# Long convolution with a dense layer: product on VectorE, shared buffers in both stages of the convolution, wider weight split

## The chip, the core and the metric

The kernel runs on one core of a Trainium2 chip. Five engines work side by side, each through its own list of instructions in order: TensorE (PE, matrix products, with the loading of weights shown apart as PEld), VectorE (DVE), ScalarE (ACT), GpSimd (POOL) and SyncE (SP), which here only starts transfers (DMA). An instruction waits until what it needs is there, and everything behind it on its engine waits with it. The metric is the device time of one execution in microseconds, less is better.

## The reference

Two steps, with a batch of 4, a sequence S of 12480 and a width D of 128. The convolution runs along the sequence with a filter that a small network makes from position embeddings; the dense layers (called MoE in the names) follow on each of the 49920 tokens, with 2048 inner columns.

```python
h_filt = (np.maximum(pos_emb @ w1, 0.0) @ w2) * np.exp(-0.01 * pos)[:, None]
u = x * v
Uf = np.fft.rfft(u, n=2 * S, axis=1)
Hf = np.fft.rfft(h_filt, n=2 * S, axis=0)
y = np.fft.irfft(Uf * Hf[None], n=2 * S, axis=1)[:, :S, :]
a = (x * y).reshape(B * S, D)
g = np.maximum(a @ w_in, 0.0) ** 2
return g @ w_out
```

Inputs and result are float32; the weights of the dense layers arrive as 64-bit floats, whose bits the kernel splits on the chip into a high and a low part that TensorE can multiply.

## The kernel before

The transform over 90 x 128 points is done as matrix products, in four quarters q of 32 channels each. A quarter has two stages.

**Stage one** has 20 chunks c. The first 16 hold signal: the tiles x and v (98 x 1024, 392 KB each) are loaded by SP (`load_c`, L161, with x in 4 and v in 3 buffers), POOL multiplies them (`prep`, L176), DVE makes the sums and differences u (L179), PE multiplies u by the transform matrix (`s1_quad`, pss, L196, 32 rows of the profile a chunk), and ACT copies the result to P (L199, two a chunk). The last 4 chunks hold the filter, loaded as four tiles f from the DRAM tensor fd (L166), whose parts DVE and ACT copy to u (L185). `load_c` runs three chunks ahead, `prep` two chunks, across the border of a quarter too.

In quarter 0 the filter itself is made beside chunks 0 to 7: four groups a chunk, each with the product psm1 (L125) on 64 partitions, a relu on ACT (L127), the product psm2 (L134), the window on DVE (ft, L136) and sums and differences on DVE and POOL (feo, L145), which `store_f` stores to fd.

Beside stage one the 64-bit weights are split (`weights`): a part of CW = 256 columns (tile raw, L228) is loaded by SP, DVE takes it apart in 14 operations on tiles cv (L233 to L250), and wst goes to the DRAM tensor wd (L252). Sixteen parts make four a quarter. The generator runs in pieces, one in each of several chunks.

**Stage two** has 30 steps z a quarter. PE multiplies P by wt (psx, L270; wt loaded by SP, L258), ACT copies a part (hs, L274), DVE multiplies (two tiles t, L278), POOL makes the two halves of y (L286, L287), PE multiplies again (psc, L295), ACT copies (ci, L297), DVE makes cs (L299, L300), and SP stores it to the DRAM tensor cd (L301). The second half of a step (`i2`, from psc on) runs two steps late, through the list todo; the last two of a quarter run after the next quarter's stage one.

**Stage three** goes back through the transform (psy, pst) and through the dense layers (psh, L467, and pso, L493). It takes the time from about 842 us on. What it needs first (the inverse transform's iwt, x3, the weights wi and wo from wd) is loaded during the last second stage.

The order on each engine is written by hand (a manual schedule): instructions stand there as the Python code emits them. Tiles come from pools; a tile that takes a used buffer waits for the last user of that buffer.

Of the kernel before, what the change touches and what calls it, by code (L numbers as in the profile page):

```python
# [66 lines left out]
CW = 256  # L67
# [12 lines left out]
def conv_moe(ctx, tc, xc, vc, xg, pos, win, w1, w2, ew, fw, ident_d, sw, iw, iw0, w_in, w_out, out):  # L80
# [23 lines left out]
    with ExitStack() as c1:  # L104
        big = c1.enter_context(tc.tile_pool(name="big", bufs=1, side="right"))
        low = ExitStack()
        s1 = low.enter_context(tc.tile_pool(name="s1", bufs=3))
# [7 lines left out]
        def load_f(i):  # L115
            if i < NG // FG:
                pt = wf.tile([FO, FG, G2 * RF], F32, tag="pos", name="pt")
                sp.dma_start(pt, pos[i])
                sf["pos", i] = pt

        def filt(g):
            if g >= NG:
                return
            ps = psM.tile([FO, G2 * RF], F32, tag="m1", name="psm1")
            pe.matmul(ps, lhsT=w1_sb, rhs=sf["pos", g // FG][:, g % FG], start=True, stop=True)  # L125
            h1 = wf.tile([FO, G2, RF], F32, tag="h1", name="h1")
            act.activation(h1.rearrange("p a b -> p (a b)"), ps, AF.Relu)  # L127
            sf["h", g] = h1

        def filt2(g):  # L130
            h1 = sf.pop(("h", g))
            ps = psM.tile([RF, G2, D], F32, tag="m2", name="psm2")
            for j in range(G2):
                pe.matmul(ps[:, j], lhsT=h1[:, j], rhs=w2_sb, start=True, stop=True)  # L134
            ft = wf.tile([RF, G2, D], F32, tag="ft", name="ft")
            dve.tensor_tensor(  # L136
                ft, ps, win_sb[:, G2 * g : G2 * g + G2].unsqueeze(2).broadcast_to([RF, G2, D]), op=ALU.mult
            )
            i, j = g // FG, 2 * (g % FG)
            if j == 0:  # L140
                sf["eo", i] = wf.tile([RF, 2, Q, 2 * FG, QC], F32, tag="feo", name="feo")
            ft = ft.rearrange("p j (q d) -> p j q d", q=Q)
            for e, op in enumerate((ALU.add, ALU.subtract)):
                fe = sf["eo", i][:, e, :, j : j + 2].rearrange("p q j d -> p j q d")
                (dve, pool)[e].tensor_tensor(fe, ft[:, :2], ft[:, 2:], op=op)  # L145

        def store_f(i):
            fe = sf.pop(("eo", i))
            for e in range(2):
                sp.dma_start(fd[:, :, e, 2 * FG * i : 2 * FG * (i + 1)].rearrange("n q j d -> n q (j d)"),  # L150
                             fe[:, e].rearrange("n q j d -> n q (j d)"))


        def load_c(g):
            q, c = divmod(g, NC)
            if q >= Q or c > NU:
                return
            if c < NU:
                for n, src in enumerate((xc, vc)):
                    ch[g, n] = s1.tile([R1, 8 * N2], F32, tag="xv"[n], name="xv"[n], bufs=4 - n)  # L160
                    sp.dma_start(ch[g, n], src[q, c])  # L161
                return
            for e in range(2):
                for h in range(2):
                    t = s1.tile([R1, 8 * N2], F32, tag="xv"[e], name=f"f{e}", bufs=4 - e)
                    sp.dma_start(t[:RF], fd[:, q, e, 32 * h : 32 * (h + 1)].rearrange("n j d -> n (j d)"))  # L166
                    ch["f", e, h] = t[:RF].rearrange("n (j d) -> n d j", d=QC)

        def prep(g):
            q, c = divmod(g, NC)  # L170
            if q >= Q:
                return
            u = s1.tile([R1, 8, N2], F32, tag="u", name="u")
            if c < NU:
                x, v = (ch.pop((g, n)) for n in range(2))
                pool.tensor_tensor(x, x, v, op=ALU.mult)  # L176
# [3 lines left out]
            else:  # L180
                d = 8 * (c - NU)
                for e, copy in enumerate((dve.tensor_copy, act.copy)):
                    for h in range(2):
                        j = e * H2 + 32 * h
                        copy(u[:RF, :, j : j + 32], ch["f", e, h][:, d : d + 8])  # L185
# [22 lines left out]
        nums = const.tile([128, 16], U32, tag="num", name="nums")  # L208
# [4 lines left out]
        def weights(i):  # L213
# [12 lines left out]
            else:  # L226
# [4 lines left out]
                t, sg, m, rest = (s1.tile([128, CW], U32, tag=f"cv{n}", name=f"cv{n}", bufs=1) for n in range(4))  # L231
                shl, shr = ALU.logical_shift_left, ALU.logical_shift_right
                dve.scalar_tensor_tensor(t, wh, 1, num(21), op0=shl, op1=shr)  # L233
# [3 lines left out]
                dve.scalar_tensor_tensor(sg, wh, 31, num(31), op0=shr, op1=shl)  # L237
                dve.scalar_tensor_tensor(sg, t, 23, sg, op0=shl, op1=ALU.bitwise_or)
# [4 lines left out]
                dve.scalar_tensor_tensor(rest, wl, 3, num(9), op0=shl, op1=shr)  # L243
                dve.tensor_tensor(rest, rest, sg, op=ALU.bitwise_or)
                fr, fm = rest.bitcast(F32), m.bitcast(F32)
# [15 lines left out]
        def s2(z):  # L261
# [14 lines left out]
            for c in range(2):  # L276
                t = s2p.tile([N2, 6, B, QC], F32, tag=f"t{c}", name=f"t{c}", bufs=2)
# [373 lines left out]
```

## Time and profile before

| | us |
|---|---|
| median of 3 runs | 3168.01 (3164.02 to 3176.44) |
| the profiled execution | 3183.8 |
| its span in the profile | 3181.9 |
| quarter 0: stage one, stage two | 0 to 181.8, to 270.3 |
| quarter 1 | to 357.2, to 448.1 |
| quarter 2 | to 532.3, to 623.2 |
| quarter 3 | to 706.5, to 812.8 |
| first products of stage three | about 842 |

The borders are read from the timeline of PE, where pss gives way to psx and psc, and back. Busy shares over the whole span: PE 96%, DVE 76%, ACT 66%, POOL 27%. These are averages over stages with different limits, so the stages are looked at one by one. In the rows of the profile each group has its line, engine, operation, the tile written and the tiles read, the shape, the count, the busy time and mean duration, and the idle time of the engine just ahead of it with what ended it. In a table of stretches each engine has its busy time and, in brackets, its number of instructions; PEclk is the clock that TensorE was granted, as a share of the full one.

### The profile page before, as it was taken

How to read it: one execution, taken by the hardware profiler on the slowest of the kernel's cores; microseconds unless marked ns; L12 is line 12 of the kernel's file. 1: busy time of each engine (PE TensorE's matmuls, PEld its weight loads, DVE VectorE, ACT ScalarE, POOL GpSimd, SP SyncE). 2: the span in 40 equal slices, each digit the busy share in tenths (PEclk: the TensorE clock that was granted, in tenths of full speed). 3: DMA queues.
4: the chain of work that ended last, by engine and by line, in shares of the span. 5: the costliest groups of instructions: out<-in, count | busy, mean ns of one | idle time of the engine just before them, and what ended most of it. 6: DMA issues, size and time to landing. Idle time of an engine off the chain costs nothing.

```text
span 3181.9 us, 42191 instructions
## 1 busy us (share of the span) xinstructions
PE 3058.0 (96%) x15370; PEld 2472.3 (78%) x15370; DVE 2433.7 (76%) x2853; ACT 2097.4 (66%) x2634; POOL 852.2 (27%) x662
## 2 busy tenths in 40 slices
PE   8997988978799999999999999999999999999999
PEld 5676767767688888888888888888888888888887
DVE  3688888888677777777777777777777777777776
ACT  2243434343477777777777787777777777777776
POOL 3456464646221111121121121111211121111210
PEclk7798999989899999999999999999999999999999
DMA  5567676757421112221121221221221222211110
GB/s 149 160 183 204 182 205 188 208 167 243 118 73 58 51 58 63 66 61 58 51 63 58 67 59 51 58 63 56 70 58 52 58 63 64 62 58 52 58 36 14
DMA packets 205807, 291.75 MB, mean 92 GB/s; under 512 B 13470, under 2 KB 131616, under 8 KB 205088
## 3 DMA queue, kind: packets, MB, share of 16 engines
q1 hardware_dynamic: 196240, 262.96, 28.5%
q0 software_dynamic: 9360, 26.10, 3.0%
q8 instruction: 122, 2.00, 0.3%
q14 instruction: 85, 0.70, 0.1%
HBM read 205.77 MB, written 83.23 MB: 91 GB/s over the span
## 4 chain that ended last, share of the span: by engine, by line
PE 88%; DVE 6%; DMA 3%; issue 1%; ACT 1%; POOL 1%; SPq 0%; DVEq 0%; POOLq 0%; ACTq 0%
PE psh L467 34%; PE pso L493 33%; PE psx L270 6%; PE psy L436 5%; PE psc L295 5%; PE pss L196 3%; DVE u L179 2%; PE pst L453 1%; PE psm L134 1%; PE psm L125 1%; DMA f<-fd 1%; DMA wt<-in_sw_dram 1%; DMA raw<-in_w_out_dram 1%; DVE cv L237 0%; ACT P L199 0%
## 5 line engine op out<-in xcount | busy, mean ns | idle before, releaser
L88 DVE TENSOR_TENSOR glo<-gt,ghi 128x1024 fp32r<-128x1024 f32 (+1 forms) x784 | 1090.5, 1391 | 60.6 <-DVE ghi L479 1.4
L470 ACT ACTIVATE rt<-psh 128x1024 f32<-128x1024 f32 (+1 forms) x784 | 800.8, 1021 | 401.1 <-PE psh L467 386.4
L479 DVE CAST ghi<-gt 128x1024 fp32r<-128x1024 f32 (+1 forms) x784 | 540.9, 690 | 470.6 <-ACT gt L477 469.6
L493 PE MATMUL pso<-ghi,wo 128*128 128x512 f32 (+1 forms) x3136 | 858.0, 390 | 0.0
L467 PE MATMUL psh<-xhi,wi 128*128 128x512 f32 (+1 forms) x3136 | 856.8, 395 | 0.6 <-ACT xhi L85 0.4
L477 ACT ACTIVATE gt<-rt 128x1024 f32<-128x1024 f32 (+1 forms) x784 | 829.3, 1058 | 23.8 <-DVE glo L88 0.4
L88 POOL TENSOR_TENSOR clo<-ca,chi 128x512 fp32r<-128x512 f32 x126 | 225.3, 1788 | 1746.7 <-ACT chi L85 1184.8
L493 PEld LDWEIGHTS pso<-ghi,wo 128*128 128x128 f32 x3136 | 588.4, 188 | 124.8
L467 PEld LDWEIGHTS psh<-xhi,wi 128*128 128x128 f32 x3136 | 580.2, 188 | 120.8 <-ACT xhi L85 0.6
L493 PE MATMUL pso<-glo,wo 128*128 128x512 f32 (+1 forms) x1568 | 500.7, 390 | 0.0
L467 PE MATMUL psh<-xlo,wi 128*128 128x512 f32 (+1 forms) x1568 | 484.4, 390 | 0.0
L467 PEld LDWEIGHTS psh<-xlo,wi 128*128 128x128 f32 x1568 | 294.7, 188 | 65.4
L493 PEld LDWEIGHTS pso<-glo,wo 128*128 128x128 f32 x1568 | 294.2, 188 | 64.8
L196 PE MATMUL pss<-e_sb,u 98*64 98x180 f32 (+1 forms) x2560 | 262.2, 361 | 72.1 <-DVE u L179 66.4
L196 PEld LDWEIGHTS pss<-e_sb,u 98*64 98x64 f32 (+1 forms) x2560 | 215.7, 157 | 117.8 <-issue 52.5
L199 ACT COPY P<-pss 128x720 f32<-128x720 f32 x160 | 126.6, 796 | 205.3 <-PE pss L196 205.3
L278 DVE TENSOR_TENSOR t<-psx,hs 128x768 f32<-128x768 f32 x240 | 218.3, 953 | 46.7 <-PE psc L295 33.8
L270 PEld LDWEIGHTS psx<-P,wt 128*128 128x128 f32 x1440 | 212.7, 188 | 45.6 <-issue 12.5
L270 PE MATMUL psx<-P,wt 128*128 128x160 f32 x1440 | 221.8, 302 | 13.4 <-DMA wt<-in_sw_dram 8.0
L274 ACT COPY hs<-psx 128x192 f32<-128x192 f32 x240 | 65.2, 323 | 236.2 <-PE psx L270 234.4
L176 POOL TENSOR_TENSOR x<-x,v 98x1024 f32<-98x1024 f32 x64 | 160.6, 2511 | 143.7 <-DMA v<-in_vc_dram 103.1
L88 POOL TENSOR_TENSOR clo<-cb,chi 104x512 fp32r<-104x512 f32 x126 | 166.4, 1321 | 111.4 <-ACT chi L85 95.0
(54 smaller groups left out, 2180.5 us busy)
## 6 DMA issues: line engine op xcount, KB each, us to landing
cd<-cs SPq DMA_DIRECT2D x120, 384.0 KB
cb<-cd SPq DMA_DIRECT2D x128, 208.0 KB
iwt<-in_iw_dram POOLq DMA_DIRECT2D x65, 392.0 KB, 3.4
x<-in_xc_dram SPq DMA_DIRECT2D x64, 392.0 KB
v<-in_vc_dram SPq DMA_DIRECT2D x64, 392.0 KB
x<-in_x_dram SPq DMA_DIRECT2D x128, 196.0 KB
out_dram<-os SPq DMA_DIRECT2D x48, 512.0 KB
wt<-in_sw_dram SPq DMA_DIRECT2D x120, 192.0 KB
```

The lines of the kernel that those rows point to most:

```text
L88: eng.tensor_tensor(dst, src, hi.bitcast(F32), op=ALU.subtract)
L176: pool.tensor_tensor(x, x, v, op=ALU.mult)
L196: pe.matmul(pv[p, a], lhsT=u[:rows, 4 * h + a, p], rhs=e_sb[:rows, e : e + 2].rearrange("n c k -> n (c k)"), start=True, stop=True)
L270: pe.matmul(xp[:, 3 * c + i, :SIG], lhsT=wt[:, i], rhs=sl["P"][:, c * (N1 // 2) + kp, :, t], start=True, stop=True)
L278: dve.tensor_tensor(t, xp[:, :, : B * QC].rearrange("p m (b d) -> p m b d", b=B), hs[:, c].rearrange("p r k d -> p (r k) d").unsqueeze(2). ...
L295: pe.matmul(cp[c], lhsT=f_sb[:, c], rhs=y[:, c], start=True, stop=True)
L436: pe.matmul(yp, lhsT=lhs, rhs=rhs, start=n == 0, stop=n == len(ops) - 1)
L467: pe.matmul(ps[:, j, :n], lhsT=wi[wp][:, f * 128 : (f + 1) * 128], rhs=bl[b][dp][:, j * n : (j + 1) * n], start=(wp, dp) == TERMS[0], stop ...
L470: act.activation(rt, ps[:, :, :n], AF.Relu)
L477: act.activation(gt, rt, AF.Square)
L479: dve.tensor_copy(hi, gt)
L493: pe.matmul(un["o"][j], lhsT=wo[tm[0]][:, f], rhs=g[tm[1]][:, j], start=f == 0 and tm == TERMS[0], stop=f == NF - 1 and tm == TERMS[-1])
```

## The change

Six edits, all ahead of stage three:

1. The product x * v goes from POOL to DVE.
2. The tiles x, f0, t0 and t1 share five buffers (tag "x"), and v, f1, y and cs share five others (tag "v"), from a pool that lives through both stages. u has 4 buffers where it had 3.
3. `load_c` runs up to five chunks ahead within a quarter. The next quarter's chunks 0 to 2 are loaded in steps 24, 26 and 28 of stage two, and its first two preparations stand in steps 26 and 28. Before, they stood in the last chunks of stage one.
4. The filter takes two groups at a time on 128 partitions: w1 stands twice on the diagonal of a 128 x 128 matrix, and psm2 reads the upper and the lower half of h1 in turn. feo has one buffer for each of sum and difference.
5. CW = 512: eight parts, two a quarter, 13 operations on DVE and the high part's copy on ACT, in pieces of one or two operations over eight chunks.
6. All four u copies of a filter chunk are ACT's. The transfers for stage three are placed anew: ident, wi and the first iwt at the start of the last second stage, wo between the first two loads of stage three; iwt has 2 buffers where it had 3.

```diff
-CW = 256
+CW = 512
...
-        s1 = low.enter_context(tc.tile_pool(name="s1", bufs=3))
+        s1 = low.enter_context(tc.tile_pool(name="s1", bufs=4))
+        mix = c1.enter_context(tc.tile_pool(name="mix", bufs=5, side="right"))
+        def buf(tag, name):
+            return mix.tile([128, 8 * N2], F32, tag=tag, name=name)
...
-            ps = psM.tile([RF, G2, D], F32, tag="m2", name="psm2")
+            ps = [psM.tile([RF, G2, D], F32, tag="m2", name="psm2") for _ in range(2)]
             for j in range(G2):
-                pe.matmul(ps[:, j], lhsT=h1[:, j], rhs=w2_sb, start=True, stop=True)
+                for h in range(2):
+                    r = slice(h * FO, (h + 1) * FO)
+                    pe.matmul(ps[h][:, j], lhsT=h1[r, j], rhs=w2_sb[r], start=True, stop=True)
...
-                    ch[g, n] = s1.tile([R1, 8 * N2], F32, tag="xv"[n], name="xv"[n], bufs=4 - n)
+                    ch[c, n] = buf("xv"[n], "xv"[n])[:R1]
...
-                pool.tensor_tensor(x, x, v, op=ALU.mult)
+                dve.tensor_tensor(x, x, v, op=ALU.mult)
...
-                for e, copy in enumerate((dve.tensor_copy, act.copy)):
+                for e in range(2):
                     for h in range(2):
                         j = e * H2 + 32 * h
-                        copy(u[:RF, :, j : j + 32], ch["f", e, h][:, d : d + 8])
+                        act.copy(u[:RF, :, j : j + 32], ch["f", e, h][:, d : d + 8])
...
                 dve.tensor_tensor(m, m, sg, op=ALU.bitwise_or)
-                dve.scalar_tensor_tensor(rest, wl, 3, num(9), op0=shl, op1=shr)
-                dve.tensor_tensor(rest, rest, sg, op=ALU.bitwise_or)
+                yield
+                act.copy(hi, fm)
+                dve.scalar_tensor_tensor(t, wl, 3, num(9), op0=shl, op1=shr)
+                dve.tensor_tensor(t, t, sg, op=ALU.bitwise_or)
+                yield
...
-                dve.tensor_tensor(hi, fm, fm, op=ALU.max)
...
-                t = s2p.tile([N2, 6, B, QC], F32, tag=f"t{c}", name=f"t{c}", bufs=2)
+                t = buf("x", f"t{c}")[:, : 6 * B * QC].rearrange("p (m b d) -> p m b d", m=6, b=B)
...
-            y = s2p.tile([N2, 2, 3 * B * QC], F32, tag="y", name="y")
+            y = buf("v", "y")[:, : 6 * B * QC].rearrange("p (c w) -> p c w", c=2)
...
-            cs = s2p.tile([N2, 2, 3 * B * QC], F32, tag="cs", name="cs")
+            cs = buf("v", "cs")[:, : 6 * B * QC].rearrange("p (c w) -> p c w", c=2)
...
+                for c in (3, 4):
+                    load_c(q, c)
                 for c in range(NC):
-                    g = q * NC + c
-                    load_c(g + 3)
-                    if c % 5 == 0:
-                        last, part, wpart = part, weights(wpart), wpart + 1
-                    if c % 5 == 1:
-                        next(last, 0)
-                    if c % 5 < 4:
-                        next(part, 0)
+                    if c + 5 <= NU:
+                        load_c(q, c + 5)
+                    if c % 10 == 0:
+                        part, wpart = weights(wpart), wpart + 1
+                    next(part, 0)
...
-                    prep(g + 2)
-                    s1_quad(g, 0)
-                    s1_quad(g, 1)
+                    if c + 2 < NC:
+                        prep(c + 2)
+                    s1_quad(c, 0)
+                    s1_quad(c, 1)
...
+                    if q < Q - 1 and s in (26, 28):
+                        prep(s // 2 - 13)
+                    if q < Q - 1 and s in (24, 26, 28):
+                        load_c(q + 1, s // 2 - 12)
...
             load3(0)
+            for i in range(2):
+                sp.dma_start(wo[i].rearrange("p c d -> p (c d)").bitcast(F32), wd[1, i])
             load3(1)
```

How this moves instructions is seen on three engines at the border from quarter 0's second stage to quarter 1's first stage, and in that stage's last chunks. The first is DVE at the border, before: t and cs belong to the last steps of stage two, u is chunk 2, cv the first weight part.

```order
255 L278 TENSOR_TENSOR t_2066<-psx,hs 128x768
256 L278 TENSOR_TENSOR t_2068<-psx,hs 128x768
257 L299 TENSOR_TENSOR cs<-psc_2073,ci 128x384
258 L300 TENSOR_TENSOR cs<-psc_2073,ci 128x384
259 L179 TENSOR_TENSOR u<-x 98x8x64 x2
260 L233 SCALAR_TENSOR_TENSOR cv_2119<-raw,nums 128x256
261 L235 SCALAR_TENSOR_TENSOR cv_2119<-cv_2119,nums 128x256
```

The same border on DVE after the change; the first two rows are the preparation of chunk 1, the rows ahead of cv that of chunk 2.

```order
237 L180 TENSOR_TENSOR x<-x,v 98x1024
238 L183 TENSOR_TENSOR u<-x 98x8x64 x2
239 L284 TENSOR_TENSOR t_1981<-psx,hs 128x768
240 L284 TENSOR_TENSOR t_1983<-psx,hs 128x768
241 L305 TENSOR_TENSOR cs<-psc_1988,ci 128x384
242 L306 TENSOR_TENSOR cs<-psc_1988,ci 128x384
243 L180 TENSOR_TENSOR x<-x,v 98x1024
244 L183 TENSOR_TENSOR u<-x 98x8x64 x2
245 L237 SCALAR_TENSOR_TENSOR cv_2042<-raw,nums 128x512
246 L238 SCALAR_TENSOR_TENSOR cv_2042<-cv_2042,nums 128x512
```

A preparation now stands between the last steps of stage two, and the first use of raw stands on DVE ahead of every preparation from chunk 3 on.

The second place is SP at the same border, before: the store of step 27, then chunk loads with raw among them. The waits name the counters of engines and of DMA queues that the transfer waits for.

```order
141 L301 DMA cd<-cs 256x3x128 [waits DMAHW4_49,DVE_49]
142 L161 DMA x<-in_xc_dram 98x1024 [waits DMAHW5_49]
143 L161 DMA v<-in_vc_dram 98x1024 [waits DMAHW6_49,Activation_49]
144 L228 DMA raw<-in_w_in_dram 128x512 [waits DMAHW7_49]
145 L161 DMA x<-in_xc_dram 98x1024 [waits DMAHW0_49]
146 L161 DMA v<-in_vc_dram 98x1024 [waits DMAHW1_49,Pool_49]
```

And SP there after the change.

```order
144 L307 DMA cd<-cs 256x3x128 [waits DMAHW7_49,DVE_49]
145 L168 DMA x<-in_xc_dram 98x1024 [waits DMAHW0_49,Pool_49]
146 L168 DMA v<-in_vc_dram 98x1024 [waits DMAHW3_49,DMAHW1_49,Activation_49]
147 L168 DMA x<-in_xc_dram 98x1024 [waits DMAHW2_49]
148 L168 DMA v<-in_vc_dram 98x1024 [waits DMAHW5_49,DVE_49]
149 L168 DMA x<-in_xc_dram 98x1024 [waits DMAHW4_49,Pool_49]
150 L168 DMA v<-in_vc_dram 98x1024 [waits DMAHW7_49]
151 L231 DMA raw<-in_w_in_dram 128x1024 [waits DMAHW6_49]
```

Raw, twice as long, has moved from behind one pair of chunk loads to behind three; the wait of row 148 on DVE is for the product of chunk 2.

The third place is ACT in the last chunks of that first stage, before: u copies of the filter and P copies.

```order
110 L199 COPY P<-pss 128x4x90x2 x28
111 L185 COPY u<-f_2514 96x8x32
112 L185 COPY u<-f_2516 96x8x32
113 L199 COPY P<-pss 128x4x90x2 x2
114 L185 COPY u<-f_2514 96x8x32
115 L185 COPY u<-f_2516 96x8x32
```

And after the change, where wst is the high part of the weight split.

```order
106 L202 COPY P<-pss 128x4x90x2 x18
107 L189 COPY u<-f_2339 96x8x32
108 L189 COPY u<-f_2341 96x8x32
109 L189 COPY u<-f_2343 96x8x32
110 L189 COPY u<-f_2345 96x8x32
111 L202 COPY P<-pss 128x4x90x2 x2
112 L249 CAST wst<-cv_2349 128x512
113 L189 COPY u<-f_2339 96x8x32
```

Four u copies stand ahead of each pair of P copies, where two stood.

More of the change, by code (lines that the diff above doesn't have):

```diff
@@ L147, in store_f @@
         def store_f(i):
-            fe = sf.pop(("eo", i))
-            for e in range(2):
+            for e, fe in enumerate(sf.pop("eo")):
                 sp.dma_start(fd[:, :, e, 2 * FG * i : 2 * FG * (i + 1)].rearrange("n q j d -> n q (j d)"),
[L151 to L157, printed above, removed]
+                             fe.rearrange("n q j d -> n q (j d)"))
@@ L207, in conv_moe @@
         NUM = (0, 9, 21, 31, 254)
-        nums = const.tile([128, 16], U32, tag="num", name="nums")
+        nums = const.tile([128, 24], U32, tag="num", name="nums")
         def num(v):
@@ L322, in conv_moe @@
                 pool.memset(nums[:, i : i + 1], v)
-            w1_sb = load("w1", [FO, FO], w1)
+            w1_sb = load("w1", [2 * FO, 2 * FO], w1)
             load_f(0)
-            w2_sb = load("w2", [FO, D], w2)
+            w2_sb = load("w2", [2 * FO, D], w2)
+            load_f(1)
             win_sb = load("win", [RF, N2], win)
-            load_c(0)
-            load_f(1)
+            load_c(0, 0)
             e_sb = load("e", [R1, 3, N1], ew)
-            load_c(1)
-            load_c(2)
+            load_f(2)
+            load_c(0, 1)
+            load_c(0, 2)
             f_sb = load("f", [N2, 2, N2], fw)
-            ident = load("id", [R1, R1], ident_d)
             filt(0)
-            for g in range(2):
-                prep(g)
+            for c in range(2):
+                prep(c)
             part, wpart = iter(()), 0
@@ L380, in conv_moe @@
                     todo.append(z)
-                    if q == Q - 1 and 4 <= s < 8:
-                        h, i = divmod(s - 4, 2)
-                        sp.dma_start((wi[i], wo[i].rearrange("p c d -> p (c d)"))[h].bitcast(F32), wd[h, i])
-                    if q == Q - 1 and s in (8, 9):
-                        load3_w(s - 8)
+                    if q < Q - 1 and s in (26, 28):
+                        prep(s // 2 - 13)
+                    if q < Q - 1 and s in (24, 26, 28):
+                        load_c(q + 1, s // 2 - 12)
             while todo:
                 i2(todo.pop(0))
+    w4 = ctx.enter_context(tc.tile_pool(name="p3w4", bufs=2))
+    wo = [w4.tile([128, NF, D], F32R, tag=f"wo{i}", name=f"wo{i}", bufs=1) for i in range(2)]
     io3 = ctx.enter_context(tc.tile_pool(name="p3io", bufs=2, side="right"))
+    st3 = {}
     def load3(p):
-        if p not in st3:
-            load3_w(p)
         ca = io3.tile([128, 2, W], F32, tag="ca", name="ca")
@@ L402, in load3 @@
             sp.dma_start(cb[q * CB : (q + 1) * CB], im[M:])
-        st3[p].update(ca=ca, cb=cb)
+        wt = w0
+        if p:
+            wt = [w4.tile([128, 2, 4, R1], F32R, tag="w", name="iwt")]
+            pool.dma_start(wt[0], iw[p])
+        xt = w4.tile([R1, 2, W], F32, tag="x", name="x3")
+        for j, n2 in enumerate(_pair(p)):
+            sp.dma_start(xt[:, j], xg[n2])
+        st3[p] = dict(ca=ca, cb=cb, w=wt, x=xt)
     with ExitStack() as c3:
@@ L503, in conv_moe @@
             load3(0)
+            for i in range(2):
+                sp.dma_start(wo[i].rearrange("p c d -> p (c d)").bitcast(F32), wd[1, i])
             load3(1)
@@ L623 @@
     moe = [a.view(np.int64) if a.dtype == np.float64 else a for a in moe]
+    w1b = np.zeros((2 * FO, 2 * FO), np.float32)
+    w1b[:FO, :FO] = w1b[FO:, FO:] = w1
     ins = dict(
```

112 lines of the change are left out of this document (52 added, 60 removed).

## The prediction

> **What bounds the kernel now.** I read the page first, then the table of stretches cut at the borders of the stages, then groups and timeline of the stretches that the change touches.
>
> ```profile
> span 3181.9 us, 42191 instructions
> PE 88%; DVE 6%; DMA 3%; issue 1%; ACT 1%; POOL 1%; SPq 0%; DVEq 0%; POOLq 0%; ACTq 0%
> core 0: us, PE busy (x) PEld busy (x) DVE busy (x) ACT busy (x) POOL busy (x), PEclk, DMA share, GB/s
> 48.00:92.00 44.00, 44.00 (x182) 27.64 (x182) 14.52 (x27) 8.26 (x14) 16.40 (x14) 0.50 0.46 131
> 92.00:137.00 45.00, 43.42 (x240) 28.93 (x238) 23.55 (x42) 10.86 (x18) 20.99 (x18) 0.70 0.51 147
> 137.00:181.80 44.80, 34.84 (x370) 28.50 (x367) 39.06 (x57) 23.17 (x32) 16.82 (x7) 0.92 0.67 200
> 270.30:357.20 86.90, 64.22 (x642) 53.88 (x641) 75.80 (x99) 34.97 (x47) 43.65 (x19) 0.80 0.68 202
> 357.20:448.10 90.90, 89.89 (x484) 73.17 (x482) 81.52 (x119) 31.58 (x91) 56.56 (x58) 1.00 0.67 183
> 448.10:532.30 84.20, 63.96 (x642) 53.68 (x641) 72.66 (x98) 35.04 (x47) 42.65 (x19) 0.84 0.71 208
> 623.20:706.50 83.30, 62.80 (x641) 52.30 (x641) 70.16 (x96) 35.26 (x47) 38.06 (x17) 0.86 0.63 183
> 706.50:812.80 106.30, 94.26 (x490) 74.10 (x488) 84.63 (x124) 32.39 (x93) 60.73 (x63) 1.00 0.75 224
> ```
>
> PE ends the chain, but from 842 us on nothing is changed. What can move is the first 842 us: four first stages (0 to 181.8 with the filter, then the rows of 86.9, 84.2 and 83.3 us) and four second stages. The second stages are PE's (89.89 busy of 90.9). The first stages are not: PE works 64.22 of 86.9 us, DVE 75.80.
>
> **Product on VectorE.** Part of DVE's 75.80 us is a wait that counts as work:
>
> ```profile
> 283.57 0.42 DVE L237 SCALAR_TENSOR_TENSOR cv<-raw,nums 128x256 uint32<-128x256 uint32 x1
> 284.36 2.56 DVE L239 SCALAR_TENSOR_TENSOR cv<-raw,nums 128x256 uint32<-128x256 uint32 x1
> 284.07 2.57 POOL L176 TENSOR_TENSOR x<-x,v 98x1024 f32<-98x1024 f32 x1 [1.62 <-DMA v<-in_vc_dram]
> L176 POOL TENSOR_TENSOR x<-x,v 98x1024 f32<-98x1024 f32 x16 | 41.3, 2583 | 41.0 <-DMA v<-in_vc_dram 36.7 <-DVE cv L249 3.4 <-DVE cv L244 0.8
> 276.07 1.29 DVE L179 TENSOR_TENSOR u<-x 98x512 f32<-98x512 f32 x2 [3.55 <-POOL x L176]
> 1505.61 1.23 DVE L88 TENSOR_TENSOR glo<-gt,ghi 128x1024 fp32r<-128x1024 f32 x1
> 1506.78 0.69 DVE L498 COPY os<-pso 128x512 f32<-128x512 f32 x1
> ```
>
> The same kind of cv operation takes 0.42 us alone and 2.56 beside POOL's product. A DVE operation on two 1024-wide inputs took 1.23 us with POOL idle, so a preparation (product and both u) costs DVE 1.23 + 1.29 = 2.52 us, with no POOL left in stage one. A weight operation on 512 columns lies between 0.42 (256 wide) and 1.23 (1024); I take 0.69, the row of width 512. Two parts of 13 come to 18 us a quarter, against four parts of 14 before at 0.42, 23.5 us without waits. DVE's work for a first stage is then 14 preparations, 35.3 us, and 18: 53 us. By that alone stage one would lose some 25 us. The queue order takes it back.
>
> **Stage one of quarters 1 to 3**, from its old start (t = 0):
>
> ```profile
> 266.80 1.82 DVE L278 TENSOR_TENSOR t<-psx,hs 128x768 f32<-128x768 f32 x2 [0.22 <-PE psc L295]
> ...
> 269.77 1.82 DVE L278 TENSOR_TENSOR t<-psx,hs 128x768 f32<-128x768 f32 x2 [0.22 <-PE psc L295]
> 271.97 0.55 DVE L300 TENSOR_TENSOR cs<-psc,ci 128x384 f32<-128x384 f32 x1
> L286 POOL TENSOR_TENSOR y<-t,t 128x384 f32<-128x384 f32 x29 | 29.0, 1002 | 35.6 <-DVE t L278 34.2 <-PE psx L270 1.4
> 274.70 0.38 SPq L228 DMA_DIRECT2D raw<-in_w_in_dram  x1
> 280.99 1.75 DVE L233 SCALAR_TENSOR_TENSOR cv<-raw,nums 128x256 uint32<-128x256 uint32 x1 [3.62 <-DMA raw<-in_w_in_dram]
> GB/s 180 201 234 279 268 272 270 279 74 43 321 6 268 223 223 298 307 264 173 204 145 4 0 190 252 293 319 309 172 4 40 288 248 350 255 166 0 185 239 247
> ```
>
> 1. DVE ended stage two at 272.5, t = 2.2. Preparations 0 and 1 now stand in stage two, where DVE waits only 0.22 us in a step, and beside POOL's y (1.00 us each); I charge one y each: 2 x 3.5 = 7.0. DVE ends at 9.2 and preparation 2 at 11.7. Without meeting a y it is 2 us less, with two y each 2 us more. The buffers that y, cs and v now share make the y of the last steps wait for a cd store issued one or two steps (2.97 us, start to start of the t rows) before; I cost that at nothing, and 3 us a stage if the store is late.
> 2. The first raw part is twice as large and stands on SP behind the cd store of step 27, six chunk loads, and v waits for product 2. Store and loads (0.38 + 6 x 0.40 MB) and raw (0.52 MB) are 3.3 MB; at the 270 GB/s of the slices that is 12.2 us from about t = 5, and some 3.5 us for issues and waits: 21. Before, it landed 6.3 us after issue (274.70 to 280.99). Bounds: no stall, or 12 us. I take 9.3, since SP is in order. Behind it on DVE stands every later preparation; PE has two chunks in hand.
> 3. Chunks 1 to 7: 13 x 0.69 and 7 x 2.52 = 26.6, to 47.6. Three without weights: 55.2.
> 4. The second raw part stands behind the v that waits for product 12 (t = 53.9): issue 54.3, landing 60.6 by the same 6.3 us, 5.4 lost. Bounds 0 and 9.
> 5. Product 14, for which the last f load waits: 60.6 + 4 x 0.69 + 2.52 + 1.23 = 67.1. Half the f loads are then already in; the last takes about 3.7 (between 1.5 us of its own 0.38 MB at 270 GB/s and the 5.9 below): 70.8.
> 6. The tail behind the last f:
>
> ```profile
> 336.07 1.25 SPq L166 DMA_DIRECT2D f<-fd  x3
> 342.93 0.63 ACT L185 COPY u<-f 96x256 f32<-96x256 f32 x1 [0.46 <-DMA f<-fd]
> 357.14 1.24 PE L295 MATMUL psc<-y,f_sb 128*128 128x384 f32 x3
> L185 ACT COPY u<-f 96x256 f32<-96x256 f32 x8 | 4.9, 651 | 0.5 <-DMA f<-fd 0.5
> L199 ACT COPY P<-pss 128x720 f32<-128x720 f32 x39 | 31.0, 799 | 51.2 <-PE pss L196 51.2
> ```
>
> It took 14.3 us (342.93 to 357.2), ACT nearly without a break: four times two u copies of 0.65 and some twelve P copies of 0.80 are 14.8. Now ACT makes all four u copies of a chunk: 8 x 0.65 = 5.2 more, 19.5. The stage ends at 90.3, against 86.9, 84.2 and 83.3: +3.4, +6.1, +7.0, **+16.5** together. Deeper loads don't enter: y(28) and y(29) hold two of the five v slots until stage two goes on, so the v of a chunk still waits for the product three chunks earlier.
>
> **Quarter 0.**
>
> ```profile
> 92.45 0.86 PE L125 MATMUL psm<-pt,w_sb 64*64 64x384 f32 x2
> 93.24 1.11 PE L134 MATMUL psm<-w_sb,h 64*96 64x128 f32 x8
> 118.46 1.54 PE L125 MATMUL psm<-pt,w_sb 64*64 64x384 f32 x2
> 119.93 2.02 PE L134 MATMUL psm<-w_sb,h 64*96 64x128 f32 x8
> ```
>
> PE is full from 48 to 137 us (44.00 and 43.42 busy), DVE is not: here only PE's work counts. A psm1 of a group takes 0.79 us at full clock (start to start) and 1.47 at the granted half. Two of four a chunk go: 1.6 or 2.9 us, at the mix of these rows (granted 0.50, then 0.70) about 2.4; seven such chunks **-17**. With the clock at full throughout, these would fall by 36 in all; if the pairs of psm2 wait for ft, since one pair takes both buffers, by 5. Behind them DVE (39.06 of 44.8) sets the pace: by steps 3 to 6, six preparations, a raw stall and the longer tail take about 40: **-5** (0 to -9).
>
> The single feo buffer makes the first feo of a chunk wait for the fd store of the chunk before; a chunk's pss, 2.67 to 4.3 us (rows under B), lies between, so 0.
>
> **The rest.**
>
> ```profile
> L270 PE MATMUL psx<-P,wt 128*128 128x160 f32 x1440 | 221.8, 302 | 13.4 <-DMA wt<-in_sw_dram 8.0
> ```
>
> The last second stage takes 106.3 us against 90.9: psx waits for wt loads, 8.0 of it in this group, that stand behind the bulk loads for stage three. w_out now goes elsewhere, so half of the 8.0 goes: -4. The transition pays for it: w_out (2.1 MB, 7.8 us at 270 GB/s) stands ahead of the second load of stage three, whose first pair hides more than half of it: +3. Net **-1** (-6 to +5). Fewer buffers in stage three: 0, since the chain there is PE's.
>
> **Sum**: -22 + 16.5 - 1 = -6.5 on the profiled 3183.8 (span 3181.9 and 1.9 around it). That execution lies 15.8 above the median shown, 3168.0; carried over: **3162**.
>
> **Rivals.**
> A. The raw parts land in time: the page shows up to 350 GB/s in a slice, and queues overlap. Steps 2 and 4 lose 14 of each stage, 43 in all: **3119**. Against it: DVE already waited 3.62 for a raw half as large.
> B. Slower: stalls of PE drop its clock, and it stays down.
>
> ```profile
> 270.28 5.34 PE L196 MATMUL pss<-e_sb,u 98*64 98x180 f32 x64
> 287.67 0.83 PE L196 MATMUL pss<-e_sb,u 98*64 98x180 f32 x2 [7.60 <-DVE u L179]
> 290.33 8.35 PE L196 MATMUL pss<-e_sb,u 98*64 98x180 f32 x62 [1.82 <-DVE u L179]
> ```
>
> Behind a pause of 7.60 us a chunk of 32 takes 4.3 us in place of 2.67, and from 48 to 92 us the clock was at 0.50 with PE never idle. Where a chunk costs DVE 3.9, a PE at half clock becomes the bound: 7 chunks and the tail's 4 at 0.4 to 1.1 each, about 10 us a stage, 30 in all: **3192**. It decides when the clock is still down at chunk 3.
> The Trainium skill, "TensorE: Matmul & The Clock Gate" (Part 1, HAM oscillation), says that an idle gap of over 3.4 us halves the clock and a busy window of that length restores it. The pause of 7.60 agrees; the 44 us at 0.50 without idle time do not. By the rule B would cost only a chunk or so per stall.
> C. The two psm2 of a pair stand in different halves of the array's rows, and overlap: half of the eight rows of 1.11 or 2.02, at four groups a chunk and the same mix 3.1 us a chunk, 22 in seven: **3140**. No row of before has such a pair. "TensorE: Matmul & The Clock Gate" (Part 3, row tiling) of the Trainium skill states that tiles in different row groups run concurrently; by it C holds wherever PE's matmuls, and not ft, are the limit.
> D. The change doesn't do what it says, loads five ahead: that is in the sum, and worth under 1 us a stage, since DVE's 2.52 to 3.9 us is near the 2.9 that 0.8 MB take at 270 GB/s.
>
> **How the numbers follow.** Forecast 0.40 (3146 to 3178), A 0.25, C 0.13, B 0.22. A measurement of this kernel tells 0.5%, 16 us, from no change. Faster by more: A, most of C, and 0.04 of the forecast: 0.40. Slower: most of B and 0.03: 0.21. Same: 0.39. The range cuts the outer halves of A and B: 3112 to 3192.
>
> **What would show it.** Right: stages of about 90 us with DVE waiting for raw twice, 9 and 5 us; a tail of 19 us; some 13 us a chunk in the filter. A: no raw wait, and stages near 76. B: pss chunks over 4 us through the stage. C: psm2 pairs with the same start. Wrong altogether: a second stage over 95 us, by preparations that hold up t.

## The result and the profile after

| | us |
|---|---|
| the changed kernel, median of 4 runs | 3219.94 (3214.31 to 3223.26) |
| the kernel before, median of 4 runs beside it | 3169.83 |
| ratio | 1.0156, 95% interval 1.013 to 1.0181 |
| predicted | 3162 (3112 to 3192) |
| profiled execution after, its span | 3214.3, 3212.4 |

The change makes the kernel slower by 50 us, 1.6%, and the interval leaves out 1. First the page of the changed kernel: its span, and the chain that ended last by engine and by line.

```profile
span 3212.4 us, 41665 instructions
PE 85%; DMA 6%; DVE 6%; ACT 2%; issue 1%; POOL 0%; SPq 0%; DVEq 0%; POOLq 0%; ACTq 0%
```

The chain is still PE's, but DMA has gone from 3% to 6%. The table of stretches, cut at the new borders (columns as before the change):

```profile
0.00:148.60 148.60, 103.22 (x929) 76.66 (x929) 92.74 (x138) 49.61 (x75) 37.30 (x41) 0.89 0.69 184
148.60:239.80 91.20, 87.97 (x474) 71.53 (x474) 80.26 (x116) 29.64 (x88) 55.90 (x57) 1.00 0.69 189
239.80:331.70 91.90, 62.50 (x642) 53.27 (x641) 56.59 (x75) 39.79 (x57) 4.02 (x4) 0.85 0.61 176
331.70:425.50 93.80, 90.67 (x484) 73.11 (x482) 82.31 (x120) 31.43 (x91) 55.91 (x57) 1.00 0.70 194
425.50:518.60 93.10, 63.19 (x641) 54.33 (x640) 56.58 (x75) 39.77 (x57) 4.02 (x4) 0.82 0.60 174
611.90:706.00 94.10, 62.86 (x641) 53.63 (x640) 56.62 (x75) 39.76 (x57) 4.05 (x4) 0.84 0.61 172
```

In quarter 1's first stage DVE's busy time fell from 75.80 to 56.59 us, near the 53 worked out (the window has one preparation more and the last t of stage two), and yet the stage grew by 5 us: the engine that had set its pace is now idle for over a third of it.

And stage three, which the prediction costed at nothing, in a window of 1900 us that lies wholly inside it. The number in brackets behind PE's busy time is that of its products. The kernel before:

```profile
1000.00:2900.00 1900.00, 1900.00 (x8535) 1545.16 (x8534) 1450.99 (x1553) 1470.83 (x1659) 351.74 (x260) 1.00 0.21 60
```

The changed kernel:

```profile
1000.00:2900.00 1900.00, 1900.00 (x8420) 1526.77 (x8419) 1429.84 (x1533) 1449.65 (x1637) 349.03 (x257) 1.00 0.21 59
```

PE is busy without a gap in both, at the full granted clock in both, and does 1.3% fewer products. That is the surprise of this case. Put together, from the borders on PE's timeline (the first psh stands at 835.0 us before and at 832.6 after; "about 842" ahead of the prediction is where the first pso stands):

| stage | before | after | difference | predicted |
|---|---|---|---|---|
| first stage of quarter 0 | 181.8 | 148.6 | -33.2 | -22 |
| second stages of quarters 0 to 2 | 270.3 | 278.3 | +8.0 | 0 |
| first stages of quarters 1 to 3 | 254.4 | 279.1 | +24.7 | +16.5 |
| last second stage, to the first psh | 128.5 | 126.6 | -1.9 | -1 |
| stage three | 2346.9 | 2379.8 | +32.9 | 0 |
| span | 3181.9 | 3212.4 | +30.5 | -6.5 |

The profiles differ by 30.5 us and the medians by 50: the profiled execution of before lay 14 above its median and the one after 5.6 below. Run e10 takes that up. In the same way the sum of the first 833 us, -2.4 here, is not what the medians say: run e1 puts it at +18.

### The profile page after: what moved, and what is told of

It is laid out like the page before. It is cut to its first block, busy times and chain, and to the rows that moved or that the text cites. A ratio compares the mean times of both kernels' runs of the same rounds, so it can differ in the third digit from the quotient of the medians.

```text
span 3212.4 us, 41665 instructions
## 1 busy us (share of the span) xinstructions
PE 3037.3 (95%) x15338; PEld 2448.3 (76%) x15338; DVE 2383.7 (74%) x2765; ACT 2107.2 (66%) x2658; POOL 704.1 (22%) x598
## 4 chain that ended last, share of the span: by engine, by line
PE 85%; DMA 6%; DVE 6%; ACT 2%; issue 1%; POOL 0%; SPq 0%; DVEq 0%; POOLq 0%; ACTq 0%
PE psh L470 34%; PE pso L496 34%; PE psx L276 5%; PE psy L439 4%; PE psc L301 4%; DVE x L180 2%; DVE u L183 1%; PE pst L456 1%; PE pss L199 1%; DMA f<-fd 1%; DMA raw<-in_w_out_dram 1%; ACT u L189 1%; DMA cb<-cd 1%; DMA wt<-in_sw_dram 1%; DVE t L284 1%
## 5 line engine op out<-in xcount | busy, mean ns | idle before, releaser
L496 PE MATMUL pso<-ghi,wo 128*128 128x512 f32 (+1 forms) x3136 | 871.4, 395 | 0.0
L470 PE MATMUL psh<-xhi,wi 128*128 128x512 f32 (+1 forms) x3136 | 867.0, 398 | 0.9 <-ACT rt L473 0.4
L199 PE MATMUL pss<-e_sb,u 98*64 98x180 f32 (+1 forms) x2560 | 249.7, 350 | 107.0 <-DVE u L183 84.6
L292 POOL TENSOR_TENSOR y<-t,t 128x384 f32<-128x384 f32 x120 | 120.3, 1002 | 377.2 <-DVE t L284 371.5
```

Of the source, the lines that this page charges most:

```text
L199: pe.matmul(pv[p, a], lhsT=u[:rows, 4 * h + a, p], rhs=e_sb[:rows, e : e + 2].rearrange("n c k -> n (c k)"), start=True, stop=True)
L470: pe.matmul(ps[:, j, :n], lhsT=wi[wp][:, f * 128 : (f + 1) * 128], rhs=bl[b][dp][:, j * n : (j + 1) * n], start=(wp, dp) == TERMS[0], stop ...
L496: pe.matmul(un["o"][j], lhsT=wo[tm[0]][:, f], rhs=g[tm[1]][:, j], start=f == 0 and tm == TERMS[0], stop=f == NF - 1 and tm == TERMS[-1])
```

## Experiments

Fourteen kernels ran. Each group of runs had the kernel before beside it on the same chip (medians 3168.2 for e1 to e4, 3172.2 for e5 to e8, 3183.5 for e9 to e12, 3175.6 for e13 and e14). Only e1, e4, e8, e12 and e14 have four runs; the others have one. The kernel before spread over 12 to 24 us within a group, so for single runs the lengths of the stages carry the argument, and differences of totals across groups are good to some 10 us.

### Where the weights lie: e1 to e4, e11, e12

In psh and pso the weight (a slice of wi or wo) is loaded into PE and the moving tile (xhi, xlo, ghi or glo) is streamed past it. The change moved wi and wo in SBUF, the on-chip memory where these tiles lie, and left the moving tiles where they were. By the source, the tiles ahead of the weights did it: w1 is 256 bytes a partition wider, nums 32, ident (392 bytes) no longer stands ahead of wi, and two iwt tiles and ident stand between wi and wo. What counts below is the remainder of a byte address divided by 512, called its residue; the addresses are those of the program, and no trace shows them. The moving tiles lie at residue 480. All slices of a weight tile are 512 bytes apart, so each tile has one residue: before 416 for wi and wo, after 288 for wi and 352 for wo. I give them as distances, weight less moving tile: -64 before, -192 and -128 after.

```diff
+                    w3.tile([128, 32], F32, tag="gap", name="gap3")
                     wi = [w3.tile([D, DFF], F32R, tag=f"wi{i}", name=f"wi{i}") for i in range(2)]
...
+    w4.tile([128, 368], F32, tag="gap", name="gap4", bufs=1)
     wo = [w4.tile([128, NF, D], F32R, tag=f"wo{i}", name=f"wo{i}", bufs=1) for i in range(2)]
```

> The changed kernel with two unused tiles (128 bytes a partition ahead of wi, 1472 ahead of wo) that put wi and wo at the SBUF places of the kernel before, modulo 2048 bytes. Theory P (places): stage three, where nothing else differs, is slower because the weights lie at other distances from the moving tiles; psh and pso go back from 232.6 ns a matmul (start to start) to 229.3, stage three from 2379.8 us to about 2346, the time falls by 32 to 36 us. Theory S (the stream: fewer iwt buffers, later wo, another order): the pace stays at 232 to 233 ns and the time within 5 us of the changed kernel's.

Measured: 3186.49 (3183.16 to 3189.91), 33.5 under the changed kernel. The same window of e1:

```profile
1000.00:2900.00 1900.00, 1900.00 (x8535) 1545.28 (x8535) 1451.33 (x1555) 1470.37 (x1658) 357.96 (x260) 1.00 0.21 60
```

To the product the count of the kernel before. Stage three took 2349.9 us. Nothing but places was changed, so theory S falls. Against the kernel before, 1.0067 (1.0046 to 1.0088) is left, 18 us, the share of the first 833 us.

Then each weight alone (e2 with 1920 bytes ahead of wo, e3 with 1600 and none ahead of wi):

> As the run before, but only wi at the place of the kernel before; wo stays at the changed kernel's residue. Theory P: the steps into and out of wi (psh) return to about 230 ns and some 15 us of stage three come back, if each weight's place acts alone; if it is the mixture of two residues that costs, the gain differs from half. Theory S: nothing.

> Only wo at the place of the kernel before, wi as in the changed kernel. Theory P: the 240 ns steps ahead of wo go, some 15 to 20 us of stage three come back. Theory S: nothing.

e2 took 3207.5, e3 3212.71, one run each: stage three 2369.8 and 2378.1 us, so 10.0 and 1.7 of the 33 came back, where e1 brought 29.9. The shares don't add: one weight back at -64 beside one at -128 or -192 helps little. e2's psh steps did return to 230 to 231 ns, but steps to and within pso now cost up to 234 to 235.

The other direction, on the kernel before (96 columns of float32 ahead of wi):

> The kernel before with one unused tile of 384 bytes a partition ahead of wi, so that wi and wo lie at residue 288 modulo 512 in place of 416 (the changed kernel has wi at 288 and wo at 352). Theory P: stage three becomes slower, by 10 to 35 us, the pace goes over 231 ns. Theory S: the time stays within 5 us of the kernel before.

3212.21 (3201.56 to 3227.25), ratio 1.0149 (1.0111 to 1.0186): one unused tile makes the kernel before as slow as the changed one. Its window:

```profile
1000.00:2900.00 1900.00, 1900.00 (x8394) 1517.62 (x8393) 1428.32 (x1530) 1445.38 (x1630) 344.38 (x255) 1.00 0.20 59
```

Is it the distance or the weight's own residue? In e11 the weights stayed and the moving tiles moved:

```diff
+        gp = c3.enter_context(tc.tile_pool(name="gap", bufs=1, side="right"))
+        gp.tile([128, 32], F32, tag="gap", name="gapr")
         wk = c3.enter_context(tc.tile_pool(name="p3wk", bufs=2, side="right"))
```

> The changed kernel with 128 unused bytes that move the moving tiles xhi, xlo, ghi, glo of stage three from residue 480 modulo 512 to 352; wi stays at 288 and wo at 352. If the distance between weight and moving tile counts, psh (distance -64, as in the kernel before) returns from 234 to 229 to 231 ns, and pso shows what distance 0 costs. If the weight's own residue counts, psh stays at 232 to 235 ns and the time within 5 us of the changed kernel's.

3176.92, 43 under the changed kernel (37 by the spans of the profiles), stage three 2344.7 us:

```profile
1000.00:2900.00 1900.00, 1900.00 (x8561) 1548.83 (x8560) 1454.90 (x1559) 1475.39 (x1664) 359.04 (x260) 1.00 0.21 60
```

The weights did not move, so their own residue is not what counts; the distance is. But the 128 bytes move the whole pool of stage three's working tiles, with gx, chi, rt and gt, which DVE and ACT write or read meanwhile. That it is the moving tile, and not one of these, from which the distance has to be measured is not shown. And pso at distance 0 was the fastest seen yet, 226 to 229 ns. So e12 put all at distance 0, on top of e8 (below; `[128, 48]` in place of `[128, 32]` in e1's first line):

> Run e8 with 64 bytes more ahead of wi, so that wi, wo and the moving tiles all lie at residue 480 modulo 512 (distance 0 in place of -64). If -64 is merely one good distance, the pace lies within 229 to 231 ns and the time at 3125 +- 8; if distance 0 makes both reads meet, over 232 ns and 3150 or more; if it is better, under 228 ns and 3110 or less.

3105.42 (3104.0 to 3107.98) against 3183.47, ratio 0.9753 (0.9712 to 0.9795), the fastest kernel of the study. Its window:

```profile
1000.00:2900.00 1900.00, 1900.00 (x8596) 1555.51 (x8595) 1462.16 (x1565) 1483.21 (x1670) 360.74 (x262) 1.00 0.21 60
```

All of it in one table. The ns are the mean time from one 128x512 product of stage three to the next, from the starts in the traces.

| kernel | distance of wi, wo | ns a product | products in 1900 us |
|---|---|---|---|
| e12, e14 | 0, 0 | 227.6 | 8596, 8596 |
| e11 | -64, 0 | 228.7 | 8561 |
| before, e1 | -64, -64 | 229.3 | 8535, 8535 |
| e13 | -320, -320 | 229.3 | 8536 |
| e2 | -64, -128 | 231.6 | 8455 |
| e3 | -192, -64 | 232.5 | 8426 |
| after | -192, -128 | 232.6 | 8420 |
| e4 | -192, -192 | 233.3 | 8394 |

Stage three has 9408 products of psh and pso and 650 of psy; 10058 times the 3.3 ns by which the mean step grew are 33.2 us, the 32.9 of the table of stages. (All of it is in psh and pso; the psy steps, whose weight iwt has moved too, went from 231.4 to 230.4 ns.) The chip is not the cause: stage three took 2346.8 to 2349.9 us in e1, e5 to e10 and e13, which ran on three chips with distances -64 or -320. That e13 equals the kernel before suggests that the distance counts modulo 256 bytes. Not tried: other distances, and the tiles' buffers among themselves. The weight loads themselves last 187 to 188 ns before and after. What inside the chip makes the step longer was not shown.

### The queue order in stage one: e5 to e8

The waits of the changed kernel's first stage of quarter 1 (total, times, longest):

```profile
PE pss L199 <- DVE u L183: 23.1, 6, 10.1
DVE cv L237 <- DMA raw<-in_w_in_dram: 19.7, 2, 11.1
DVE x L180 <- DMA v<-in_vc_dram: 1.1, 1, 1.1
```

DVE stands twice for raw, nearly 20 us, and hardly for v. The timeline of DVE at the border shows both places of which the prediction spoke:

```profile
239.61 1.40 DVE L180 TENSOR_TENSOR x<-x,v 98x1024 f32<-98x1024 f32 x1
241.04 1.97 DVE L183 TENSOR_TENSOR u<-x 98x512 f32<-98x512 f32 x2
242.94 1.81 DVE L284 TENSOR_TENSOR t<-psx,hs 128x768 f32<-128x768 f32 x2
...
260.45 0.69 DVE L237 SCALAR_TENSOR_TENSOR cv<-raw,nums 128x512 uint32<-128x512 uint32 x1 [11.08 <-DMA raw<-in_w_in_dram]
```

A preparation of 3.4 us stands ahead of the last t; and at 260.45, 20.7 us after the stage's border, DVE begins raw. The weight operation on 512 columns takes 0.69. ACT's timeline shows the tail:

```profile
312.50 2.30 ACT L189 COPY u<-f 96x256 f32<-96x256 f32 x4
314.69 1.49 ACT L202 COPY P<-pss 128x720 f32<-128x720 f32 x2
316.03 0.65 ACT L249 CAST wst<-cv 128x512 fp32r<-128x512 f32 x1
```

From the first u copy to the stage's end at 331.7 are 19.2 us. The three runs that follow undo one of these each, on e1.

```diff
-                for e in range(2):
+                for e, copy in enumerate((dve.tensor_copy, act.copy)):
...
-                        act.copy(u[:RF, :, j : j + 32], ch["f", e, h][:, d : d + 8])
+                        copy(u[:RF, :, j : j + 32], ch["f", e, h][:, d : d + 8])
```

> On the run e1 (weights at the places of before), only the u copies of the filter chunks shared between VectorE and ScalarE again, as before the change. Theory T (the tail is ScalarE's): the tail behind the last f falls from 19.0 to about 14.3 us, each first stage by 4 to 5 us, the time by 16 to 20 against e1. Rival: VectorE's copies queue behind its weight pieces, which wait for raw, and under 2 us a stage come back.

3178.25, 8 under e1; the first stages of quarters 1 to 3 took 90.3, 91.2 and 90.8 us against 92.9, 92.8 and 93.6. The stages fell by 1.6 to 2.8 us, between theory T (4 to 5) and its rival (under 2): the copies moved to DVE stand between weight pieces that came late behind raw, as its timeline shows.

```profile
316.45 0.68 DVE L189 COPY u<-f 96x256 f32<-96x256 f32 x2
317.04 0.69 DVE L250 SCALAR_TENSOR_TENSOR cv<-raw,nums 128x512 uint32<-128x512 uint32 x1
317.76 0.69 DVE L251 TENSOR_TENSOR cv<-cv,cv 128x512 uint32<-128x512 uint32 x1
318.37 0.65 DVE L189 COPY u<-f 96x256 f32<-96x256 f32 x2
```

Now raw:

```diff
+                    if c == 8:
+                        next(part, 0)
-                    if c % 10 == 0:
+                    if c == 8 or (c, q) == (0, 0):
                         part, wpart = weights(wpart), wpart + 1
-                    next(part, 0)
+                    if c not in (9, 10) and (c or q == 0):
+                        next(part, 0)
...
                     todo.append(z)
+                    if q < Q - 1 and s == 22:
+                        part, wpart = weights(wpart), wpart + 1
+                        next(part, 0)
```

> On e1, only the loads of raw earlier: the first of quarters 1 to 3 at step 22 of the second stage, ahead of the chunk loads, the second part of every quarter at chunk 8 in place of 10. Theory R (VectorE stands behind raw, 11.1 and 9.9 us in quarter 1): both waits go or fall under 3 us in all, and the first stages of quarters 1 to 3 fall by 12 to 18 us each (not by 21, since chunk loads then set the pace), the time by 36 to 55. Rival: the waits only turn into waits for v, and under 5 us a stage come back.

3134.45, 52 under e1. The table of stretches and the waits of e6's first stage of quarter 1:

```profile
232.90:310.70 77.80, 61.54 (x642) 50.61 (x641) 56.68 (x75) 39.85 (x57) 4.12 (x4) 0.93 0.69 202
...
DVE x L180 <- DMA v<-in_vc_dram: 3.3, 2, 2.1
DVE cv L237 <- DMA raw<-in_w_in_dram: 2.8, 1, 2.8
```

The stage falls from 92.9 to 77.8 us, and raw's two waits to 2.8: theory R. The same work with both loads of raw placed earlier, the first of them ahead of six chunk loads, brings more than the 18 us that the change costs ahead of stage three.

Then the first preparations:

```diff
+                    if c == 14 and q < Q - 1:
+                        load_c(q + 1, 0)
+                        load_c(q + 1, 1)
-                    if c + 2 < NC:
-                        prep(c + 2)
+                    if c + 2 < NC or q < Q - 1:
+                        prep((c + 2) % NC)
...
-                    if q < Q - 1 and s in (26, 28):
-                        prep(s // 2 - 13)
-                    if q < Q - 1 and s in (24, 26, 28):
-                        load_c(q + 1, s // 2 - 12)
+                    if q < Q - 1 and s == 28:
+                        load_c(q + 1, 2)
```

> On e1, only the first two preparations of the next quarter moved back from steps 26 and 28 of the second stage into the last two chunks of the first, where VectorE idles, with the loads of chunks 0 and 1 at chunk 14. Theory Q (preparations hold up t in the second stage): the second stages of quarters 0 to 2 fall by 2 to 3 us each to 88.5 to 91, and raw's wait begins earlier by some 4 us; the time falls by 6 to 15 against e1. Rival: the two chunk loads in the tail delay f, or VectorE holds up the start of the second stage, and nothing is gained.

3173.85, 13 under e1 (10 by the spans). The second stages of quarters 0 to 2 took 88.4, 90.9 and 90.9 us, to 0.1 those of before; theory Q. Its first one:

```profile
147.00:235.40 88.40, 87.20 (x472) 71.69 (x472) 78.28 (x113) 29.69 (x88) 56.66 (x58) 1.00 0.67 179
```

The first stages hardly changed (94.3, 90.9 and 92.8): in quarter 1 DVE still begins raw 21.0 us behind the border, 20.6 in e1.

> e1 with the edits of e5, e6 and e7 together: a version that should beat both kernels. If the three shares add: 3186 less 18, 45 and 10 is about 3113, ratio to before about 0.98. If the shares hide each other (all end at the same loads of v or f): 3130 to 3150.

3125.04 (3121.75 to 3125.33), ratio 0.983 (0.9784 to 0.9877); faster than both kernels. The shares (8, 52, 13) add to 73, of which 61 came: v is waited for next, 7.5 us in its first stage of quarter 1.

### Product and filter apart: e9, e10, e13, e14

```diff
-                pool.tensor_tensor(x, x, v, op=ALU.mult)
+                dve.tensor_tensor(x, x, v, op=ALU.mult)
```

> The kernel before with one edit: the product x v on VectorE. Theory L (VectorE's waits beside POOL's product are the cost): the 0.42 us weight operations stay at 0.42, and the first stages of quarters 1 to 3 fall from 85 to 87 us to 70 to 80 each, 15 to 40 us in all. Rival D (VectorE is in order, so a product that waits for its v now holds up u and weights): the stages stay within 3 us or become longer, with waits of VectorE for v in place of POOL's.

3125.31 against 3183.5 beside it, a single run: one word in the kernel before brings about what e8 brings (e14 below puts it lower by some 15 us). Its stretches are the first stages of quarters 1 to 3, then two rows of DVE's timeline there:

```profile
232.50:310.10 77.60, 61.67 (x642) 52.08 (x641) 66.37 (x116) 35.30 (x47) 3.47 (x3) 0.89 0.81 228
401.10:480.10 79.00, 65.98 (x642) 56.31 (x641) 65.77 (x115) 35.30 (x47) 3.48 (x3) 0.81 0.79 223
571.10:647.70 76.60, 61.62 (x641) 51.95 (x640) 61.46 (x110) 35.33 (x47) 3.40 (x3) 0.89 0.71 199
...
245.76 0.41 DVE L239 SCALAR_TENSOR_TENSOR cv<-raw,nums 128x256 uint32<-128x256 uint32 x1
246.10 1.22 DVE L176 TENSOR_TENSOR x<-x,v 98x1024 f32<-98x1024 f32 x1
```

The operation of line 239 that took 2.56 us beside POOL's product takes 0.41, the product itself 1.22 in place of 2.5, and DVE's busy time falls from 75.80 to 66.37 though it does POOL's work too. The three stages gained 21 us, and quarter 0's first stage ended at 144.0. Rival D falls, and theory L holds in both its signs. Not separated from DVE's waits is the product's own shorter time, with the hand-over from POOL.

> The kernel before, unchanged, for a further profile of quarter 0. Theory C (the profile that the prediction went by caught the filter at an unusually low clock): the first stage of quarter 0 ends near 161 us, as in run e4, in place of 181.8, with a span near 3160. Rival: near 182 again, and e4's 161.2 was the exception.

3189.49, quarter 0's first stage to 180.1 us. The row of the page's window from 48 to 92 us in e10, then in e4, whose program is the same up to there:

```profile
48.00:92.00 44.00, 44.00 (x186) 27.95 (x186) 14.15 (x27) 8.32 (x15) 16.25 (x13) 0.51 0.45 130
```

```profile
48.00:92.00 44.00, 42.42 (x289) 28.13 (x288) 25.20 (x50) 14.06 (x24) 23.93 (x21) 0.93 0.72 209
```

So theory C is half right: from 48 to 92 us the filter runs with the granted clock at half in two of three profiles, and at 0.93 in the third, whose first stage ends 19 to 21 us earlier (161.2). e4 ran on another chip than e10, so run and chip are not told apart here. Times of the kernel before spread from 3161 to 3195 us over the runs beside these; this is the likely reason, and it is about the 20 us by which the medians differ more than the profiles.

> The kernel before with one edit: the filter on 128 partitions (two groups at a time, feo with one buffer, the transfers of its inputs as in the changed kernel). It also moves wi and wo by 256 bytes, to residue 160 modulo 512, distance -320 to the moving tiles. Theory F (the prediction's: two psm1 a chunk less are what quarter 0 gains): its first stage ends 13 to 20 us earlier than before, at 141 to 168. Rival (run e9 has the old filter and ended at 144.0, so the product is what frees quarter 0): it ends at 158 or later. Stage three shows what distance -320 costs: 229 to 231 ns a matmul if its only bad distances are near -192 and -128, over 232 if 0 and -64 are the exceptions.

The edit is that of the change to `load_f`, `filt`, `filt2`, `store_f` and the inputs. 3156.17, the first stage of quarter 0 to 148.2 us: the filter alone is worth 13 us against e4 and 32 to 34 against the two others, theory F. Its stage three gave the row for -320 above.

> The kernel before with two edits: the product on VectorE (as e9) and 64 unused bytes ahead of wi (distance 0, as e12). Theory: the shares add, e9's 3125 less the 1.7 ns of e12 on 10058 matmuls, 17 us: 3108 +- 8, and quarter 0's first stage ends within 140 to 150 again, as in e9. Rival: e9's quarter 0 was a lucky clock, and it ends at 155 or later.

3116.11 (3112.7 to 3118.87) against 3175.63, ratio 0.9819 (0.9779 to 0.9859). Stage three took 2330.8 us, 16 under e9's, so the place adds as expected. The total lies just above the 3108 +- 8. Quarter 0's first stage ended at 156.5, as the rival said (155 or later): e9's 144.0 was a lucky clock. A group of psm2 in e9, then in e14, each with the same work:

```profile
36.98 1.11 PE L134 MATMUL psm<-w_sb,h 64*96 64x128 f32 x8
```

```profile
36.44 2.02 PE L134 MATMUL psm<-w_sb,h 64*96 64x128 f32 x8
```

From 31 us on these take 1.11 us in e9, in e14 2.02 until 45 us; the filter's third chunk begins at 47.9 us in e9 and at 57.3 in e14. Against e4's 161.2 the product is then worth 5 to 17 us in quarter 0. Both product and filter shorten quarter 0, and the changed kernel with both stands at 148.6: the second finds little left. There DVE waits for raw (11.8 us between 40 and 130 us), which may be why; no run separates it.

## Why the prediction was wrong

**The step that failed** is a half sentence under "The rest": "Fewer buffers in stage three: 0, since the chain there is PE's." The chain is PE's, but a full PE was taken for a constant one. The change moved wi and wo, and the mean step of 10058 products became 3.3 ns longer: +33 us, from e1 (gone with two unused tiles), e4 (made with one) and e11 (gone again when the working tiles follow). No rival had it. The addresses of both kernels could have been laid side by side; what a distance costs could not be read from the trace of before, which has one only.

**The rest of the sum**, -6.5 ahead of stage three, came to -2.4 in the profiles, and that nearness is luck: quarter 0 gained 11 more than predicted, against a profile with its filter at half the clock, and the first and the second stages cost 8 each more. By the medians e1, the change without the moved weights, is 18 us slower than the kernel before. So without stage three, too, the forecast would have had the wrong sign.

- *Product on VectorE*: 1.23 for the product, 0.69 for the weight operation, 53 us of work; measured 1.23, 0.69 and, with what the window has besides, 56.59. (75.80 less 53 is 22.8, not "some 25"; the sum does not use it.) That the product on POOL was a cost of the old stage is shown by e9.
- *Raw's stalls*, 9.3 and 5.4: measured 11.1 and 8.6. The mechanism, raw issued behind the chunk loads and DVE standing for it, was right, and the second was mis-sized by 3. (The two lose 14.7 a stage, 44 in three; rival A has 43.)
- *The tail*, 19.5: measured 19.2.
- *Stages of 90.3*: 91.9, 93.1 and 94.1. The step also left out what preparations cost PE inside stage two, 2.4 to 2.9 us a quarter, 8.0 in three, gone in e7; it had put that on DVE alone. The bound of 3 us was named there, for another reason.
- *Quarter 0*, -22: -33 against this profile and -13 against e4's. The base was a profile whose filter ran at half the clock. In the filter the changed kernel is quicker than the 13 us a chunk of the forecast (pss begins at 65.5, 75.0 and 83.8 us, 9 apart), and gives some of it back to raw.
- *The single feo buffer*, put at 0 because a chunk's pss lies between: POOL stood for the fd store in six chunks, and DVE's ft and PE's psm2 behind it.

```profile
POOL feo L156 <- DMA fd<-feo: 29.1, 6, 4.9
PE psm L143 <- DVE ft L147: 10.4, 11, 2.5
DVE ft L147 <- POOL feo L156: 4.9, 4, 1.7
```

So the wait that was put at nothing is there; what it adds to the time, no run shows.

- *The median*: carrying the profile's sum over to 3168 took -15.8 off as if it were spread evenly. It most likely sat in quarter 0, and the changed kernel's runs lie within 9 us, so the medians moved by 20 more than the profiles.

**Rivals.** A asked what stage one would be without raw's stalls: 76 us; e6 shows 77.8 and e8 75.6, so its price was about right and its condition not met. C held as a mechanism: two rows of PE's timeline in quarter 0, psm2 of two groups after the change,

```profile
59.87 1.12 PE L143 MATMUL psm<-w_sb,h 64*96 64x128 f32 x16
60.92 0.91 PE L132 MATMUL psm<-pt,w_sb 128*128 128x384 f32 x2
```

16 in the 1.11 us that eight took before. The Trainium skill's "TensorE: Matmul & The Clock Gate" (Part 3, row tiling) states that matmuls in different row groups run concurrently, and the trace agrees; part of what it saved went into the waits for ft above (10.4 us from 40 to 130 us), which the prediction had named as the condition. B fell. A pause costs about one chunk of pss (chunks 3 to 6 of quarter 1, then chunks 13 to 15):

```profile
263.88 11.06 PE L199 MATMUL pss<-e_sb,u 98*64 98x180 f32 x96 [10.12 <-DVE u L183]
275.22 3.16 PE L199 MATMUL pss<-e_sb,u 98*64 98x180 f32 x32 [0.28 <-DVE u L183]
...
306.27 7.92 PE L199 MATMUL pss<-e_sb,u 98*64 98x180 f32 x64 [9.43 <-DVE u L183]
315.52 2.66 PE L199 MATMUL pss<-e_sb,u 98*64 98x180 f32 x32 [1.33 <-ACT P L202]
```

Behind 9.43 us of idle time 64 rows take 7.92 in place of 5.34, and the next 32 the full-clock 2.66. Chunks 3 to 5 take 11.06 in place of 8.0, and chunk 6 takes 3.16: the pause reaches into chunk 3, as B asked, but the clock does not stay down. Here the rule that the prediction quotes from the Trainium skill, "TensorE: Matmul & The Clock Gate" (Part 1, HAM oscillation), was the better guide; it does not account for the 44 us at 0.51 with PE never idle in e10.

## What to carry to other kernels

When an edit changes pools or tile sizes, list the addresses of the operands of the bound engine's inner loop before and after: here 64 bytes of padding are worth 17 us, and a move nobody meant cost 33. Take a term that looks like "unchanged code" as unchanged only when its operands have not moved. And split a large change by single edits: one word (the product's engine) brings more than the whole change, whose other parts (raw behind six loads, copies on one engine, preparations in a full stage, moved weights) took it back.

## What the runs showed of the hardware

- The time from product to product of a gapless PE at full granted clock depends on where the weights lie in SBUF, as a distance from the moving tile and the tiles of its pool: 227.6 ns at 0, 229.3 at -64 and -320, 233.3 at -192 bytes, for 128x512 fp32r.
- Two weights that alternate, one at -64 and one at -128 or -192, keep most of the loss (231.6 in e2, 232.5 in e3); one at -64 and one at 0 keep none (228.7 in e11).
- The same instructions of the filter ran at a granted clock of 0.50 or 0.51 (before, e10) or of 0.93 (e4) from 48 to 92 us, and their stage ended some 20 us apart.
